# Attention and two gated mixers on one core: the first batch's q, k and the token weights loaded as rows, float64 weights rounded by an integer add, a new order for the first stage

## The chip, the core and the metric

The kernel runs on one core of a Trainium2 chip, as one program. A core has TensorE (PE in the profile; its weight loads are PEld), VectorE (DVE), ScalarE (ACT), GpSimd (POOL) and SyncE (SP), which here issues nearly all DMAs. Each engine works through its own instructions in the order in which they were recorded, and waits on semaphores for the others. The metric is the time of one execution on the device in microseconds (us), median of several runs.

## The reference

Eight batches, eight heads, 576 tokens, head dimension 64. Attention runs inside chunks of 64 tokens; its output is the input of a gated mixer with a token weight of 576x576, and that feeds a second mixer. Cut to what matters:

```python
scores = scale * np.matmul(q_c, k_c.transpose(0, 1, 2, 4, 3))   # chunks of 64 tokens
attn = softmax(scores); out = np.matmul(attn, v_c)
x = out.transpose(0, 2, 1, 3).reshape(B, S, H * D)
h = np.maximum(x @ w_in, 0.0); u, v = h[..., :512], h[..., 512:]
v_n = (v - mean(v)) / np.sqrt(var(v) + 1e-06)
v_s = np.einsum('ts,bsd->btd', w_spatial, v_n) + b_spatial[None, :, None]
x = (u * v_s) @ w_out
# second mixer: tokens (w_tok1, w_tok2), then channels (w_ch1, w_ch2), both with a residual
```

`w_in`, `w_out`, `w_tok1`, `w_tok2`, `w_ch1`, `w_ch2` come as float64; `q`, `k`, `v`, `w_spatial`, `b_spatial` as float32.

## The kernel before

All large products run on TensorE with each float32 operand split into a high and a low part (`split`, `to_hi` and `to_lo`), in three passes (`PASSES`). The first half of the program does, batch by batch, attention (class `Attn`) and the gated mixer (class `Gate`); the second half does the second mixer for all batches.

The order of the first half is written out by hand in tables of words, played one after the other: `FIRST` (batch 0's attention, batch 0's gate, and batch 1's attention, with the weights' conversion in between), then six times `STEADY` (gate of batch b beside attention of batch b+1), then `LAST`. One word is one step, and a step's instructions go onto their engines' queues in that order. The words that matter here, with an `a` ahead for batch 0's attention:

- `l`, `v`: loads of q and k, and of v, for a pair of heads. In the load of q and k a tile takes 32x32 blocks: 8 DMAs a pair, each with runs of 32 floats. `x`: VectorE turns the blocks (L322, L323; four instructions a pair).
- `S`, `s`, `e`, `n`, `z`, `T`, `t`, `P`, `p`, `q`: scores on TensorE (L336, L345); maximum and subtraction on VectorE (L355, L356); exponential on ScalarE (L362); sums and reciprocals on VectorE (L366 to L368); the scaling on GpSimd (L372); the turn of the probabilities on TensorE (L380) and their copy on ScalarE (L388); the product with v (L404, L412); its high part on ScalarE (L423, L433) and low part on VectorE (L425, L437).
- `Y`, `V`: v half of `x @ w_in` (L479; L508 for the last tokens). `R`, `r`, `F`, `G`, `rs`, `rq`, `N`, `i`, `Q`: its copies out of PSUM, the statistics (L531), the normalization (L545) and the high and low parts (L551, L560). `U`, `E`: the u half (L568) and its copy (L578). `W`: the product with the token weight (L591). `M`, `H`, `J`, `A`, `B`, `O`, `D`: the gate and the product with `w_out` (L601 to L625).
- `wl`, `wa`, `wm`, `we`, `wi`, `wj`, `wk`: load, conversion and split of one of the 12 float64 pieces of `w_in` and `w_out`. `cl`, `ca`, `cm`, `ce`, `cs`: the same conversion, in `STEADY`, of the 33 pieces of the second mixer's weights, which are stored as float32 for later.
- `gl`, `gt`, `gh`: load of the token weight in 32x32 blocks (L240, 20 DMAs), its turn on VectorE (L250), its split (L83 on ScalarE, L84 on GpSimd).
- `Z`: matmuls on zeros (L1124).

A float64 number is read as two 32-bit words. `conv_start` scales both on ScalarE (L143, L144), `conv_mid` shifts the exponent and puts in the sign on VectorE (L152, L154) and makes a power of two of the result's size (L156), and `conv_end` multiplies the low word by that and adds it, two GpSimd instructions (L164, L165).

`ps_mm` has two tiles of two PSUM banks each (tag `mm`), which the steps `Y`, `V`, `U`, `W`, `O` take in turn; `ps_at` has one tile each for scores (`s`), turned probabilities (`t`) and the product with v (`p`). A step that needs a tile waits until the last reader of the one before is done. The raw tiles of float64 pieces (`craw`) are two.

Of the kernel before, what the change touches and what calls it, by code (L numbers as in the profile page):

```python
# [21 lines left out]


FIRST = """
al0 ax0 Z9 wl0 al1 wa0 aS0 as0 wl1 ae0 an0 ax1 az0 wm0 aT0 we0 wa1 wm1 at0 we1 aS1 al2 Z3 as1
av0 ax2 ae1 an1 Z3 al3 az1 aP0 wi0 av1 ap0 ax3 wi1 wk0 aq0 aS2 aT1 at1 Y0 wl2 aP1 wl3 as2 ae2
wj1 aS3 av2 an2 wa2 wl4 wa3 az2 wm2 ap1 aq1 as3 we2 wa4 ae3 wm3 av3 aT2 an3 wi2 wl5 at2 Y1 aS4
gl0 as4 L0 wl6 wk2 aP2 ap2 gt0 az3 aq2 L1 ae4 aT3 at3 we3 an4 az4 wm4 x0 wa5 wm5 wi3 aP3 wk3
ap3 Y2 aT4 at4 wa6 we4 S0 aq3 aP4 Y3 we5 wm6 ap4 x1 wi4 R0 R1 wk4 aq4 r0 R3 s0 R2 r3 wl7 wi5
V2 wa7 gl1 gl2 we6 F S1 wk5 wl8 e0 wi6 U0 wm7 G r2 gl3 R4 we7 gl4 r1 r4 wa8 rs rq wk6 n0 z0 U1  # L30
E0 N0 T0 gt4 gh0 s1 i0 Q0 gt1 gh4 U2 wi7 N1 N2 t0 wk7 E1 L2 e1 i1 x2 P0 N4 i2 gh1 n1 p0 gt2 L3
U3 S2 i4 z1 wl9 Q1 gt3 gh2 N3 E2 gh3 i3 Q2 T1 Q3 Q4 W0 t1 E3 s2 wm8 wa9 W1 we8 x3 e2 M0 M1 wi8
wm9 q0 S3 W2 n2 wl10 we9 H0 wa10 W3 M2 s3 H2 wi9 J0 wl11 M3 z2 P1 S4 wk8 H1 J1 wj9 p1 q1 J2 H3
# [22 lines left out]
def attention_gmlp_mixer(  # L56
# [15 lines left out]
    nc = tc.nc  # L72
    NB, NH, S, D = q.shape
    DM = 512
    HALF = S // 2
    NF = w_ch1.shape[1] // 128
    scale = 1.0 / float(D) ** 0.5

    def f32(ap):
        return ap.bitcast(F32)  # L80

    def split(hi, lo, x, eng=nc.vector):
        nc.scalar.copy(out=hi, in_=x)  # L83
        eng.tensor_tensor(out=lo, in0=x, in1=f32(hi), op=ALU.subtract)  # L84
# [10 lines left out]
    lp = pool("left", side="left")  # L95
    rp = pool("right", side="right")
# [18 lines left out]

    def conv_load(src, raw=None):

        nr, n = src.shape[0], src.free_size()  # L120
# [16 lines left out]
    def conv_start(raw):  # L137
        if raw.dtype == F32:
            return raw, raw
        nr, n = raw.shape[:2]  # L140
        low, high = raw[:, :, 0], raw[:, :, 1]
        t = rp.tile([128, DM], F32, tag="ctmp", bufs=3, name="ctmp")[:nr, :n]
        nc.scalar.activation(out=t, in_=f32(high), func=ACTF.Copy, scale=2.0 ** -112)  # L143
        nc.scalar.activation(out=f32(low), in_=low, func=ACTF.Copy, scale=2.0 ** -52)  # L144
        return raw, t

    def conv_mid(raw, t):
        if raw.dtype == F32:
            return
        low, high = raw[:, :, 0], raw[:, :, 1]  # L150
        tu = t.bitcast(U32)
        nc.vector.tensor_scalar(  # L152
            out=tu, in0=tu, scalar1=3, scalar2=None, op0=ALU.logical_shift_left)
        nc.vector.scalar_tensor_tensor(  # L154
            out=tu, in0=high, scalar=0x80000000, in1=tu, op0=ALU.bitwise_and, op1=ALU.bitwise_or)
        nc.vector.tensor_scalar(  # L156
            out=high, in0=tu, scalar1=0xFF800000, scalar2=None, op0=ALU.bitwise_and)

    def conv_end(raw, t):

# [61 lines left out]
    ws_raw = {}  # L222

    def load_ws(m):
        if m == 4:

            both = lp.tile([128, 2, S], F32, tag="g0", bufs=1, name="ws_raw")
            ws_raw[4] = both[:, 0:1].rearrange("p o (t i) -> p o t i", i=32)
            ws_raw[5] = both[:, 1]
            for r in (64, 96):  # L230
                nc.sync.dma_start(
                    out=both[r:r + 1, 1], in_=b_sp.rearrange("(o s) -> o s", o=1))
        elif m % 2 == 0:

            ws_raw[m] = rp.tile([128, 2, 18, 32], F32, tag="xt", bufs=6, name="ws_raw")
            ws_raw[m + 1] = ws_raw[m]
        raw = ws_raw[m][:, m % 2]
        for a in range(4):
            e = 4 * m + a if m < 4 else 16 + a % 2
# [5 lines left out]
    ws_nat = {}

    def trans_ws(m):
        raw = ws_raw.pop(m)[:, m % 2].rearrange("p t i -> p (t i)")
        ws_nat[m] = lp.tile([128, S], F32, tag="x2o", bufs=2, name="ws_nat")
        nc.vector.transpose(out=ws_nat[m], in_=raw)  # L250

    def split_ws(m):
        nat = ws_nat.pop(m)
        if m < 4:
            split(ws_t[0][:, m], ws_t[1][:, m], nat, nc.gpsimd)
            return
        nc.scalar.copy(out=ws_r1, in_=nat)
        nc.vector.tensor_tensor(
            out=ws_r2[0:64], in0=nat[0:64], in1=f32(ws_r1[0:64]), op=ALU.subtract)

        bt = ws_raw.pop(5)
        nc.scalar.copy(out=ws_r2[64:65], in_=bt[64:65])
        nc.scalar.copy(out=ws_r2[96:97], in_=bt[96:97])
        nc.vector.tensor_tensor(
            out=ws_r2[96:97], in0=bt[96:97], in1=f32(ws_r2[96:97]), op=ALU.subtract)


    class Attn:
# [523 lines left out]
    raws = {}  # L792
# [345 lines left out]
    class Stream:
# [24 lines left out]
        "gl": load_ws, "gt": trans_ws, "gh": split_ws})  # L1163
# [171 lines left out]
```

## Time and profile before

| | us |
|---|---|
| median of 3 runs (1256.14 to 1257.96) | 1257.33 |
| the profiled execution: its time | 1259.11 |
| the profiled execution: its span | 1257.3 |
| busy in the span: PE / DVE / ACT / POOL | 1190.9 / 923.6 / 496.6 / 213.1 |

The span is from the first to the last instruction of the program; 1.8 us of the profiled execution lie around it, and it took 1.8 us more than the median. PE is busy for 95% of the span. The rows below are from three kinds of answers: busy time by stretch, waits, and instructions in order of time, each with its start, its duration and in brackets how long its engine had been idle and who released it.

### The profile page before, as it was taken

Reading aid. Unit: us, or ns where it says so; the run is one execution under the profiler, and the core shown is the slowest. Engines: PE = TensorE matmul, PEld = TensorE weight load, DVE = VectorE, ACT = ScalarE, POOL = GpSimd, SP = SyncE. Lnnn points to the kernel's source line nnn. Section 1 sums busy time; section 2 is a strip of 40 time slices with the busy share of each in tenths; the row PEclk is TensorE's granted clock in tenths of the full one; section 3 lists DMA queues with packets and bytes.
Section 4 is the critical chain, followed back from the end, with each engine's and each line's share of the span. In section 5 each row is a group of like instructions: output and inputs, shape, how many; then the busy total and the mean of one; then the engine's idle time right before and its main releaser. Section 6 shows DMA issues by size and latency. Waiting matters only on the chain. (4 is left out here: it accounts for less than half of the span.)

```text
span 1257.3 us, 25171 instructions
## 1 busy us (share of the span) xinstructions
PE 1190.9 (95%) x9983; PEld 1123.0 (89%) x9983; DVE 923.6 (73%) x1427; ACT 496.6 (39%) x786; POOL 213.1 (17%) x205
## 2 busy tenths in 40 slices
PE   6689999999998999999889999999998999999997
PEld 4588998989797988898779899999998999999997
DVE  6897767687776868366686776767768977877786
ACT  2564535354544536244332332232225433333331
POOL 2644122222323231105220000000005100000000
PEclk9989999999999999999999999999999999999999
DMA  9956446374739383157545665565376576666663
GB/s 162 186 111 130 86 120 116 94 172 103 183 78 202 58 195 81 72 106 210 151 139 166 183 178 180 152 171 192 141 276 202 208 208 192 185 192 196 207 212 46
DMA packets 426362, 196.16 MB, mean 156 GB/s; under 512 B 369666, under 2 KB 389570, under 8 KB 426244
## 3 DMA queue, kind: packets, MB, share of 16 engines
q1 hardware_dynamic: 421380, 193.96, 58.9%
q8 instruction: 78, 1.28, 0.4%
q10 hardware_dynamic: 4864, 0.59, 0.3%
q14 instruction: 40, 0.33, 0.1%
HBM read 123.31 MB, written 71.17 MB: 155 GB/s over the span
## 5 line engine op out<-in xcount | busy, mean ns | idle before, releaser
L953 PE MATMUL ps_c<-ub,wt 128*128 128x288 f32 x2016 | 289.3, 299 | 7.8 <-DVE u L982 2.5
L953 PEld LDWEIGHTS ps_c<-ub,wt 128*128 128x128 f32 x2016 | 278.2, 191 | 14.0 <-ACT s L985 3.6
L953 PE MATMUL ps_c<-hb,wt 128*128 128x288 f32 x2016 | 269.1, 295 | 1.6 <-DVE hb L1042 1.5
L953 PEld LDWEIGHTS ps_c<-hb,wt 128*128 128x128 f32 x2016 | 268.2, 188 | 2.4 <-DVE hb L1042 2.3
L591 PE MATMUL ps_s<-ws,vn 128*128 128x288 f32 x768 | 110.9, 301 | 2.9 <-ACT ut L578 2.8
L1041 ACT CAST hb<-h 128x1728 fp32r<-128x1728 f32 x40 | 64.8, 1638 | 123.0 <-DVE h L1034 42.9
L591 PEld LDWEIGHTS ps_s<-ws,vn 128*128 128x128 f32 x768 | 105.9, 193 | 4.5 <-ACT ut L578 4.3
L617 PE MATMUL ps_o<-g,w_out 128*128 128x288 f32 x768 | 107.6, 297 | 0.7 <-DVE w_out L190 0.7
L568 PE MATMUL ps_u<-xt,w_in 128*128 128x288 f32 x768 | 107.9, 300 | 0.0
L568 PEld LDWEIGHTS ps_u<-xt,w_in 128*128 128x128 f32 x768 | 105.5, 193 | 0.9 <-POOL w_in L190 0.2
L617 PEld LDWEIGHTS ps_o<-g,w_out 128*128 128x128 f32 x768 | 102.6, 188 | 2.5 <-DVE w_out L190 0.9
L1042 DVE TENSOR_TENSOR hb<-h,hb 128x1728 fp32r<-128x1728 f32 x40 | 78.2, 1955 | 28.9 <-ACT hb L1041 28.9
L479 PE MATMUL ps_v<-w_in,xt 128*128 128x512 f32 x384 | 94.8, 404 | 2.7 <-ACT xt L423 1.3
L479 PEld LDWEIGHTS ps_v<-w_in,xt 128*128 128x128 f32 x384 | 72.8, 192 | 21.1 <-ACT xt L423 1.5
L372 POOL TENSOR_TENSOR e<-e,sm 128x512 f32<-128x512 f32 (+1 forms) x40 | 38.9, 972 | 226.9 <-DVE sm L368 153.7
L869 PE MATMUL ps_u<-w,h 128*128 128x288 f32 x384 | 61.8, 298 | 4.5 <-DVE xh L874 4.5
L910 ACT CAST ub<-xh 128x576 fp32r<-128x576 f32 x56 | 37.4, 672 | 70.0 <-DVE xh L917 66.8
L869 PEld LDWEIGHTS ps_u<-w,h 128*128 128x128 f32 x384 | 54.7, 190 | 5.7 <-DVE xh L874 5.6
L164 POOL TENSOR_TENSOR craw<-craw 128x512 f32<-128x512 f32 (+3 forms) x41 | 40.1, 978 | 116.0 <-DVE craw L156 34.0
L911 DVE TENSOR_TENSOR ub<-xh,ub 128x576 fp32r<-128x576 f32 x56 | 43.1, 770 | 21.1 <-ACT ub L910 20.6
L811 ACT CAST xn<-nat 128x512 fp32r<-128x512 f32 x40 | 24.8, 619 | 79.2 <-DVE nat L809 74.6
L830 PE MATMUL ps_h<-xn,w 128*128 128x512 f32 x192 | 51.2, 400 | 3.5 <-ACT xn L811 3.5
(145 smaller groups left out, 1697.9 us busy)
## 6 DMA issues: line engine op xcount, KB each, us to landing
hd<-c SPq DMA_DIRECT2D x120, 288.0 KB, 2.5
h<-hd SPq DMA_DIRECT2D x40, 864.0 KB, 6.7
craw<-in_moe_w_ch_dram SPq DMA_DIRECT2D x24, 512.0 KB, 4.8
x_raw<-x2d SPq DMA_DIRECT2D x160, 64.0 KB, 2.6
qk_raw<-in_q_dram SPq DMA_DIRECT2D x128, 72.0 KB, 4.2
qk_raw<-in_k_dram SPq DMA_DIRECT2D x128, 72.0 KB, 3.1
xh<-x2d SPq DMA_DIRECT2D x16, 576.0 KB, 5.6
u2d<-xh SPq DMA_DIRECT2D x16, 576.0 KB, 3.1
```

Source lines behind the costliest of these rows:

```text
L164: nc.gpsimd.tensor_tensor(out=f32(high), in0=f32(low), in1=f32(high), op=ALU.mult)
L372: nc.gpsimd.tensor_tensor(out=e, in0=e, in1=sm.to_broadcast([128, e.shape[1], 64]), op=ALU.mult)
L479: nc.tensor.matmul(ps, lhsT=self.xt[kc][:, p, 128 * ti:128 * ti + 128], rhs=w_in_t[r][:, kc, DM:2 * DM], start=kc == 0 and n == 0, stop=kc ...
L568: nc.tensor.matmul(ps[:, h, 0:HALF], lhsT=w_in_t[r][:, kc, 128 * m:128 * m + 128], rhs=self.xt[kc][:, p, HALF * h:HALF * h + HALF], start= ...
L591: nc.tensor.matmul(ps[:, h, 0:HALF], lhsT=lhsT, rhs=rhs[:, HALF * h:HALF * h + HALF], start=n == 0, stop=n == len(ops) - 1)
L617: nc.tensor.matmul(ps[:, h, 0:HALF], lhsT=w_out_t[r][:, kc, 128 * m:128 * m + 128], rhs=self.g[p][:, kc, h], start=kc == 0 and n == 0, sto ...
L830: nc.tensor.matmul(ps[kk], lhsT=PB["w1"][r][:, m, ksl], rhs=xn[:, p], start=m == 0 and n == 0, stop=False)
L869: nc.tensor.matmul(ps, lhsT=h1[:, kk, p, 128 * m:128 * m + 128], rhs=PB["w2"][r][:, kk, HALF * h:HALF * h + HALF], start=n == 0, stop=n == 5)
L911: eng.tensor_tensor(out=lo, in0=x, in1=f32(hi), op=ALU.subtract)
L953: nc.tensor.matmul(ps, lhsT=lhsT, rhs=rhs, start=first and n == 0, stop=n == len(ops) - 1, skip_group_check=True)
L1041: nc.scalar.copy(out=hi, in_=x)
L1042: nc.vector.tensor_tensor(out=lo, in0=x, in1=f32(hi), op=ALU.subtract)
```

## The change

Three things change, all in code that runs during the first half:

1. Batch 0's q and k come as rows (`load_rows`): 128 tokens by 64 floats, runs of 64 floats, 4 DMAs a pair of heads and 2 more for the last tokens, in place of 32. The turn is made by TensorE (`turn`, eight matmuls with the identity a pair) into a `mm` tile, and ScalarE copies it out (`turned`, word `y`, two copies a pair). The later batches keep the blocks. The token weight also comes as rows (`load_ws`, 3 DMAs and 2 for the bias in place of 22); TensorE turns it (`turn_ws`, 25 matmuls in five steps into the `p` tile), and its low part is made by VectorE straight from PSUM.
2. The conversion from float64: the low word is scaled by another power of two and written as an integer, VectorE's third instruction goes, and GpSimd's two become one integer add. This touches all 45 pieces, 12 in `FIRST` and 33 in `STEADY`.
3. `FIRST` is put in a new order, and the large raw tiles (`g0`, `g1`) now hold pieces 0 to 3 rather than 4 to 7; the words `Z3` are gone. The last three lines of the table stay nearly as they were.

The core of the diff; of the table one line of each stands for all:

```diff
-al0 ax0 Z9 wl0 al1 wa0 aS0 as0 wl1 ae0 an0 ax1 az0 wm0 aT0 we0 wa1 wm1 at0 we1 aS1 al2 Z3 as1
+al0 wl0 al1 wl1 Z9 ax0 ay0 wa0 aS0 as0 ax1 al2 av0 wl2 wm0 ae0 ay1 an0 we0 az0 aS1 as1 wa1 aT0 wi0 wm1
...
-        nc.scalar.activation(out=f32(low), in_=low, func=ACTF.Copy, scale=2.0 ** -52)
+        nc.scalar.activation(out=low, in_=low, func=ACTF.Copy, scale=2.0 ** -29)
...
-        nc.vector.tensor_scalar(
-            out=high, in0=tu, scalar1=0xFF800000, scalar2=None, op0=ALU.bitwise_and)
...
-        nc.gpsimd.tensor_tensor(out=f32(high), in0=f32(low), in1=f32(high), op=ALU.mult)
-        nc.gpsimd.tensor_tensor(out=t, in0=t, in1=f32(high), op=ALU.add)
+        tu = t.bitcast(U32)
+        nc.gpsimd.tensor_tensor(out=tu, in0=tu, in1=raw[:, :, 0], op=ALU.add)
...
+    def turn_ws(m):
+        ps = ps_at.tile([128, 2, 8, 64], F32, tag="p", bufs=1, name="ps_w")
+        ps = ws_ps[m] = ps.rearrange("p a c q -> p (a c q)")
+        for c in range(5):
+            n = 128 if c < 4 else 64
+            nc.tensor.transpose(
+                ps[0:128 if m < 4 else 64, 128 * c:128 * c + n],
+                ws_rows[c][0:n, 128 * m:min(128 * m + 128, S)], ident[0:n, 0:n])
...
     def split_ws(m):
-        nat = ws_nat.pop(m)
+        ps = ws_ps.pop(m)[:, 0:S]
         if m < 4:
-            split(ws_t[0][:, m], ws_t[1][:, m], nat, nc.gpsimd)
+            split(ws_t[0][:, m], ws_t[1][:, m], ps)
...
+            for src in (q, k):    # load_rows
...
+                for h2 in range(2):
+                    nc.sync.dma_start(
+                        out=raw[:, :, h2],
+                        in_=src[b, 2 * hp + h2, 0:512, :].rearrange("(c p) d -> p c d", p=128))
...
+        def turn(self, u):
+            ps = self.qk[u] = ps_mm.tile([128, 2, 512], F32, tag="mm", name="ps_x")
...
+                        nc.tensor.transpose(
+                            ps[:, n, 128 * c:128 * c + 128],
+                            raw[n][:, c].rearrange("p h d -> p (h d)"), ident)
...
+        def turned(self, u):
...
+                nc.scalar.copy(out=ts[n], in_=ps[:, n])
...
-        if 4 <= i < 8:
+        if i < 4:
```

Where this moves instructions, at three places. First, VectorE in the third round of `STEADY` (the first where both pieces are whole ones of 128x512), from the conversion of two pieces (`ctmp`, `craw`) to the statistics of v. Before:

```order
L152 TENSOR_SCALAR ctmp<-ctmp 128x512
L154 SCALAR_TENSOR_TENSOR ctmp<-craw,ctmp 128x512
L156 TENSOR_SCALAR craw<-ctmp 128x512
L152 TENSOR_SCALAR ctmp<-ctmp 128x512
L154 SCALAR_TENSOR_TENSOR ctmp<-craw,ctmp 128x512
L156 TENSOR_SCALAR craw<-ctmp 128x512
L531 BN_STATS st<-v_3249 128x6
```

The same place now:

```order
L153 TENSOR_SCALAR ctmp<-ctmp 128x512
L155 SCALAR_TENSOR_TENSOR ctmp<-craw,ctmp 128x512
L153 TENSOR_SCALAR ctmp<-ctmp 128x512
L155 SCALAR_TENSOR_TENSOR ctmp<-craw,ctmp 128x512
L588 BN_STATS st<-v_3227 128x6
```

Two of six instructions ahead of the statistics are gone; nothing else moved there.

Second, TensorE in `FIRST` from the end of batch 0's v product (`ps_v`) to its u product (`ps_u`); `ps_s` are batch 1's scores. Before:

```order
L508 MATMUL ps_v<-w_in_84,xt 128x512
L508 MATMUL ps_v<-w_in_85,xt 64x512
L508 MATMUL ps_v<-w_in_84,xt 128x512
L508 MATMUL ps_v<-w_in_85,xt 64x512
L508 MATMUL ps_v<-w_in_84,xt 128x512
L508 MATMUL ps_v<-w_in_85,xt 64x512 x2
L508 MATMUL ps_v<-w_in_84,xt 128x512
L336 MATMUL ps_s<-qkT_706,qkT_703 64x64 x16
L568 MATMUL ps_u<-xt,w_in_84 128x288 x2
```

The same place now:

```order
L246 MATMUL ps_w<-ident,ws_rows 128x128 x4
L246 MATMUL ps_w<-ident,ws_rows 128x64
L391 MATMUL ps_s<-qkT_665,qkT_662 64x64 x16
L565 MATMUL ps_v<-w_in_84,xt 128x512
L565 MATMUL ps_v<-w_in_85,xt 64x512
L565 MATMUL ps_v<-w_in_84,xt 128x512
L565 MATMUL ps_v<-w_in_85,xt 64x512
L565 MATMUL ps_v<-w_in_84,xt 128x512
L565 MATMUL ps_v<-w_in_85,xt 64x512 x2
L565 MATMUL ps_v<-w_in_84,xt 128x512
L246 MATMUL ps_w<-ident,ws_rows 128x128 x4
L246 MATMUL ps_w<-ident,ws_rows 128x64
```

Two of the five turns of the token weight (`ps_w`) stand here, and batch 1's first scores come ahead of L565 rather than, as before, ahead of the end of the v product.

Third, ScalarE at the same place of `FIRST`: the copies of v out of PSUM (`v_162` to `v_166`, `v_sum`), a piece's high part (`w_in_84`), the token weight's (`ws_88`). Before:

```order
L526 ACTIVATE v_162<-ps_v 128x512
L526 ACTIVATE v_163<-ps_v 128x512
L526 ACTIVATE v_165<-ps_v 128x512
L526 ACTIVATE v_164<-ps_v 128x512
L187 CAST w_in_84<-ctmp 128x4x128
L143 ACTIVATE ctmp<-wu_raw 128x512
L144 ACTIVATE wu_raw<-wu_raw 128x512
L517 COPY v_sum<-ps_v 64x512
L518 COPY v_sum<-ps_v 64x512
```

The same place now:

```order
L583 ACTIVATE v_162<-ps_v 128x512
L583 ACTIVATE v_163<-ps_v 128x512
L83 CAST ws_88<-ps_w 128x576
L583 ACTIVATE v_165<-ps_v 128x512
L185 CAST w_in_84<-ctmp 128x4x128
L574 COPY v_sum<-ps_v 64x512
L575 COPY v_sum<-ps_v 64x512
L417 ACTIVATE e<-e 128x512
L583 ACTIVATE v_164<-ps_v 128x512
```

The copy of `v_164`, which is the last reader of its `mm` tile, was fourth in a row and now stands behind a piece's high part, the copies for `v_sum` and an exponential.

## Rows read from the trace of the kernel before

**Rows 1.** Busy time by stretch: PE, PEld, DVE, ACT, POOL, clock, DMA, GB/s.

```profile
0.00:54.40 54.40, 35.85 (x401) 26.73 (x401) 40.33 (x75) 21.45 (x40) 25.48 (x27) 0.94 0.93 171
54.40:81.90 27.50, 20.16 (x208) 17.81 (x208) 26.23 (x52) 20.34 (x34) 14.81 (x13) 0.97 0.87 168
119.20:255.00 135.80, 135.12 (x1405) 124.68 (x1394) 92.81 (x200) 59.89 (x120) 24.89 (x30) 1.00 0.51 111
255.00:525.00 270.00, 257.77 (x2627) 238.64 (x2627) 196.64 (x379) 124.69 (x228) 75.29 (x66) 0.99 0.56 129
```

**Rows 2.** What TensorE waited for from 119.2 to 525 us.

```profile
PE ps_t L380 <- POOL e L372: 4.4, 4, 1.1
PE ps_s L336 <- DVE last L323: 4.4, 4, 1.8
```

**Rows 3.** In order of time, STEADY's fourth round: start, duration, engine, instruction.

```profile
316.58 0.69 DVE L154 SCALAR_TENSOR_TENSOR ctmp<-craw,ctmp 128x512 uint32<-128x512 uint32 x1
...
325.29 1.43 DVE L154 SCALAR_TENSOR_TENSOR ctmp<-craw,ctmp 128x512 uint32<-128x512 uint32 x1
...
326.83 0.43 DVE L156 TENSOR_SCALAR craw<-ctmp 128x512 uint32<-128x512 uint32 x1
...
327.34 1.15 POOL L164 TENSOR_TENSOR craw<-craw 128x512 f32<-128x512 f32 x1 [1.16 <-DVE craw L156]
...
327.63 1.41 DVE L154 SCALAR_TENSOR_TENSOR ctmp<-craw,ctmp 128x512 uint32<-128x512 uint32 x1
...
329.14 1.34 DVE L156 TENSOR_SCALAR craw<-ctmp 128x512 uint32<-128x512 uint32 x1
...
330.40 0.69 DVE L531 BATCH_NORM_STATS2 st<-v 128x6 f32<-128x512 f32 x1
...
331.74 1.30 POOL L165 TENSOR_TENSOR ctmp<-ctmp,craw 128x512 f32<-128x512 f32 x1
...
336.47 1.15 PE L336 MATMUL ps_s<-qkT,qkT 64*64 64x64 f32 x32 [1.47 <-DVE last L323]
...
338.73 0.66 PE L380 MATMUL ps_t<-ident,e 128*128 128x128 f32 x4 [1.10 <-POOL e L372]
```

**Rows 4.** TensorE in order of time, the third round, same place.

```profile
268.12 1.15 PE L336 MATMUL ps_s<-qkT,qkT 64*64 64x64 f32 x32 [0.25 <-DVE last L323]
```

**Rows 5.** TensorE in order of time, FIRST.

```profile
2.69 4.21 PE L1124 MATMUL ps_w<-zeros 128*128 128x512 f32 x9 [2.69 <-DVE zeros L1118]
...
7.87 1.97 PE L336 MATMUL ps_s<-qkT,qkT 64*64 64x64 f32 x32 [0.98 <-DVE qkT L322]
...
51.34 3.06 PE L479 MATMUL ps_v<-w_in,xt 128*128 128x512 f32 x12
...
72.59 0.69 PE L404 MATMUL ps_p<-aT,vt 64*64 64x64 f32 x32 [0.95 <-ACT aT L388]
...
80.68 1.11 PE L380 MATMUL ps_t<-ident,e 128*128 128x128 f32 x4 [2.70 <-POOL e L372]
81.91 5.68 PE L591 MATMUL ps_s<-ws,vn 128*128 128x288 f32 x24
...
87.95 3.36 PE L591 MATMUL ps_s<-ws,vn 128*128 128x288 f32 x24
```

**Rows 6.** Groups by line and form, 0 to 119.2 us: busy, mean ns.

```profile
L322 DVE STREAM_TRANSPOSE qkT<-qk_raw 128x512 f32<-128x512 f32 x18 | 12.5, 693 | 5.0 <-DMA qk_raw<-in_k_dram 2.9 <-DMA qk_raw<-in_q_dram 2.2
L143 ACT ACTIVATE ctmp<-craw 128x512 f32<-128x512 f32 x8 | 5.4, 674 | 17.7 <-DMA craw<-in_moe_w_in_dram 14.1 <-DMA craw<-in_moe_w_out_dram 3.6
L388 ACT COPY aT<-ps_t 128x512 f32<-128x512 f32 x8 | 4.6, 581 | 3.3 <-PE ps_t L380 3.3
L250 DVE STREAM_TRANSPOSE ws_nat<-ws_raw 128x576 f32<-128x576 f32 x5 | 3.8, 763 | 2.0 <-DMA ws_raw<-in_moe_w_spatial_dram 2.0
L601 DVE TENSOR_TENSOR ut<-ps_s,ut 128x576 f32<-128x576 f32 x4 | 3.0, 748 | 2.9 <-PE ps_s L591 2.9
L355 DVE TENSOR_REDUCE mx<-ps_s 128x8 f32<-128x512 f32 x8 | 5.4, 676 | 2.0 <-PE ps_s L336 1.9
```

More of the change, by code (lines that the diff above doesn't have):

```diff
@@ L220, in attention_gmlp_mixer @@
                   for c in range(0, w.shape[1], DM)]
[L222 to L239, printed above, removed]
-            nc.sync.dma_start(
-                out=raw[32 * a:32 * a + 32],
-                in_=w_sp[:, 32 * e:32 * e + 32].rearrange("(t j) i -> j t i", j=32),
-            )
@@ L245, in attention_gmlp_mixer, with load_ws @@
[L245 to L250, printed above, removed]
+    ws_rows = {}
+    def load_ws(i):
+        if i < 2:
+            t = rp.tile([128, 2, S + 64], F32, tag="xt", bufs=6, name="ws_rows")[:, :, 0:S]
+            nc.sync.dma_start(
+                out=t, in_=w_sp[256 * i:256 * i + 256].rearrange("(c p) n -> p c n", p=128))
+            for c in range(2):
+                ws_rows[2 * i + c] = t[:, c]
+            return
+        ws_rows[4] = lp.tile([128, S], F32, tag="x2o", bufs=2, name="ws_rows")
+        nc.sync.dma_start(out=ws_rows[4][0:64], in_=w_sp[512:576])
+        for r in (64, 96):
+            nc.sync.dma_start(
+                out=ws_rows[4][r:r + 1], in_=b_sp.rearrange("(o s) -> o s", o=1))
@@ L254, in split_ws @@
         if m < 4:
-            split(ws_t[0][:, m], ws_t[1][:, m], nat, nc.gpsimd)
+            split(ws_t[0][:, m], ws_t[1][:, m], ps)
             return
-        nc.scalar.copy(out=ws_r1, in_=nat)
+        for h in range(2):
+            nc.scalar.copy(out=ws_r1[64 * h:64 * h + 64], in_=ps[0:64])
         nc.vector.tensor_tensor(
-            out=ws_r2[0:64], in0=nat[0:64], in1=f32(ws_r1[0:64]), op=ALU.subtract)
-        bt = ws_raw.pop(5)
+            out=ws_r2[0:64], in0=ps[0:64], in1=f32(ws_r1[0:64]), op=ALU.subtract)
@@ L300, in load_qk, with load_rows @@
             self.raw[hp] = raws
+        def load_rows(self, hp):
+            b = self.b
+            raws = []
+            for src in (q, k):
+                raw = rp.tile([128, 18, 32], F32, tag="raw", bufs=4, name="qk_rows")
+                raw = raw.rearrange("p t i -> p (t i)")[:, 0:512].rearrange(
+                    "p (c h d) -> p c h d", c=4, h=2)
+                for h2 in range(2):
+                    nc.sync.dma_start(
+                        out=raw[:, :, h2],
+                        in_=src[b, 2 * hp + h2, 0:512, :].rearrange("(c p) d -> p c d", p=128))
+                raws.append(raw)
+            self.raw[hp] = raws
+            if hp == 3:
+                raw = lp.tile([128, S], F32, tag="x2o", bufs=2, name="qk_rows")
+                raw = raw[:, 0:512].rearrange("p (h d) -> p h d", h=8)
+                for n, src in enumerate((q, k)):
+                    nc.sync.dma_start(
+                        out=raw[64 * n:64 * n + 64],
+                        in_=src[b, :, 512:576, :].rearrange("h p d -> p h d"))
+                self.raw[4] = raw
@@ new lines, in turn @@
+        def turn(self, u):
+            ps = self.qk[u] = ps_mm.tile([128, 2, 512], F32, tag="mm", name="ps_x")
+            raw = self.raw.pop(u)
+            for n in range(2):
+                if u < 4:
+                    for c in range(4):
+                        nc.tensor.transpose(
+                            ps[:, n, 128 * c:128 * c + 128],
+                            raw[n][:, c].rearrange("p h d -> p (h d)"), ident)
+                else:
+                    r = slice(64 * n, 64 * n + 64)
+                    for hp in range(4):
+                        nc.tensor.transpose(
+                            ps[:, n, 64 * hp:64 * hp + 64],
+                            raw[r, 2 * hp:2 * hp + 2].rearrange("p h d -> p (h d)"),
+                            ident[r, r])
@@ new lines, in turned @@
+        def turned(self, u):
+            ps = self.qk.pop(u)
+            if u == 4:
+                for n in range(2):
+                    nc.scalar.copy(
+                        out=self.last[n].rearrange("p h d -> p (h d)"), in_=ps[:, n, 0:256])
+                return
+            self.qk[u] = ts = [rp.tile([128, 512], F32, tag=f"qkT{n}", bufs=2, name=f"qkT{n}")
+                               for n in range(2)]
+            for n in range(2):
+                nc.scalar.copy(out=ts[n], in_=ps[:, n])
@@ L456, in ops @@
                        q=lambda u: self.put(u, 1))
+            if self.b == 0:
+                ops.update(x=self.turn, y=self.turned)
             return {pre + n: fn for n, fn in ops.items()}
```

27 lines of the change are left out of this document (16 added, 11 removed).

## The prediction

> **What bounds the kernel now.** I read busy time by stretch first. From 119.2 to 255 us TensorE is busy for 135.1 of 135.8 us: nothing that frees another engine can be seen there. From 255 to 525 us it idles for 12.2 us, and in the first stage, up to 54.4 us and from there to 81.9 us, for 18.6 and 7.3 us [rows 1]. So the change can act at two places: the first stage, and the last four rounds of STEADY. Then the waits of the second: of its idle time, 4.4 us are for VectorE's turn of q and k, and 4.4 us for GpSimd's scaling, four times each, once a round [rows 2]. Then the instructions around one such wait, in order of time. The reader is to see a row of VectorE work without a gap: from the second L154 at 327.63 over L156 at 329.14 to L531 at 330.40 and on to the turn that releases TensorE at 336.47, 1.47 us late; then TensorE waits 1.10 us more for the scaling that follows [rows 3]. In this place VectorE sets TensorE's time.
>
> In the first stage no engine is full up to 54.4 us (VectorE 40.3, TensorE 35.9, ScalarE 21.5); the chain from step to step and the DMAs bound it, ScalarE alone waiting 14.1 us for pieces of w_in [rows 1, 6]. From 54.4 to 81.9 us VectorE is busy for 26.2 of 27.5 us [rows 1]: there it is the bound.
>
> **The conversion in STEADY.** 33 times VectorE loses L156 and GpSimd's L164 and L165 become one add. What a round gains is the shift of L531. The first L154 ends at 326.72 in both. Before, L156 follows, and L164 can begin only behind it, at 327.34; the second L154 stands beside it and takes 1.41 us, not the 0.69 it takes alone; the second L156 stands beside L165 and takes 1.34 us, not 0.43 [rows 3]. Now the add begins at 326.8. Its price isn't in the trace: GpSimd has no integer instruction. The nearest rows are L165 (1.30, the same tiles and strides, an add) and L164 (1.04 to 1.15); the far end is that it costs as much as both together, 2.35. I take 1.30, as the row with the same operation and operands. Then it ends at 328.1, the second L155 needs the 0.55 us that its forerunner needed behind L164's end (328.49 to 329.04), and L531 begins at 328.75, not 330.40: 1.65 us. TensorE's two waits in that round add up to 2.57 us, so all of it counts. In the third round the two waits are 0.25 and, as in every round, 1.1 us [rows 2, 4]: at most 1.35 there. The rounds five and six have the other 4.9 us of the 8.8 [rows 2], more than a shift of 1.65 each can use up. Sum: 1.35 + 3 x 1.65 = **6.3 us**. At 1.04 a piece it would be 7.1; at 2.35 L531 moves by only 0.6, and the sum is 2.4. What is late next: the scaling, still by some 0.9 us a round.
>
> That the add blocks VectorE is the row's reading: 1.41 beside a GpSimd instruction, 0.69 without. The Trainium skill ("GPSIMD Engine Reference", section Key points) says that GpSimd shares its SBUF interfaces with VectorE, and that instructions with two SBUF inputs or in a two-port mode contend; the trace agrees. By that rule the add holds L155 back as L164 did, which the sum has in it; without it L155 would end 0.7 us sooner, and the sum would be 8.
>
> ScalarE's L145 now writes integers. No row has that; L144 reads them at the speed of L143 (0.67). Bounds: 0.58, as a plain copy, and 1.35, twice as much; I take 0.67 and no change, since ScalarE is busy for 125 of 270 us there [rows 1, 6].
>
> **The first stage, to the end of the v product.** It ends at 54.40 before [rows 5]. Now: the nine matmuls on zeros stay and end at 6.9; the first turn is eight matmuls at the half-clock price of L380 (1.11 for four), to 9.1; a copy of 0.58; first scores at 9.9, two us later than the 7.87 of before [rows 5, 6]. From pair to pair: scores 1.15, maximum and subtraction 2 x 0.68, exponential about a copy's 0.6, two copies 1.16, and one piece's two scalings 1.35, which stand between them on ScalarE: 5.6 us [rows 3, 6]. So the fourth pair's scores are at 26.7. To the first Y: 1.15 + 1.36 + 0.6, two half copies 0.6, two scalings 1.35 and a cast 0.6, a copy 0.58, P 0.69 and the last scores 0.6: 7.5, at 34.2. From there TensorE has all it needs: four Y of 3.06 and two T and two P in between, about 2.2: the end is at 48.7, **5.7 us ahead**. The DMAs aren't in this chain: q and k need 18 DMAs, not 32, the token weight 5, not 22, and ScalarE's 14.1 us of waiting go [rows 6]. Of the moved loads, piece 6 stands ahead of batch 1's second pair on SP's queue and waits there for a raw tile, until piece 4 is converted at about 45; the pair's blocks are wanted at 60.
>
> **From there to the gate's W.** W begins at 81.91 before, 27.5 us behind the v product [rows 5]. TensorE's 20.2 us grow by 25 turns at 0.165 (L380 at full clock, 0.66 for four: 4.1) and by batch 1's first scores (1.15), which were earlier before: 25.5 [rows 1, 3]. If nothing waited, W would begin at 74.2. But VectorE's 26.2 us hardly shrink: less five turns at 0.76 (3.8) and one L156 (0.4), plus four low parts from PSUM at 0.75 as L601 (3.0) and the blocks of one more pair (1.8): 26.8 [rows 3, 6]. 1.5 of it can be done under the v product; the next VectorE instruction waits for the first turn and its high part on ScalarE, until 50.2. Five more times VectorE waits for ScalarE, which itself stands behind something: behind the v_164 copy, behind the square root, behind the table load of the exponential. I price each at 1.3, a copy and a cast with their handoffs: 6.5. So 50.2 + 25.3 + 6.5 = 82.0, then scores and T (1.8) and W at **84, 2 us late**. Where the waits queue up: on ScalarE a cast waits for GpSimd's add of piece 5, and behind it stand the v_sum copies and v_164, whose tile the first U needs: TensorE idles some 3 us there, and some 4 before the last U, whose tile ScalarE frees behind the cast of piece 7.
>
> Behind W: its 5.68 us ran at half clock, against 3.36 for the next one [rows 5]; TensorE had idled 2.7 us before it. If the clock is up, 2.3 come back; as the idle times are as long now, I count half, 1.2. The first stage: 2.1 - 1.2, **1 us later** than before. Bounds: 7.7 sooner (nothing waits), and 11 later (below).
>
> The Trainium skill speaks against the turns ("TensorE: Matmul & The Clock Gate", Part 4: PE-mode transpose): about 275 ns for one in a kernel's context. The rows have four in 0.66 us, so 0.165 each. By the page's figure the 25 turns would be 6.9 and not 4.1, an estimate, and W 2.8 us later.
>
> **The sum**, against the profiled execution's own 1259.11 us: - 6.3 + 1 = 1253.8. That execution was 1.8 above the median of 1257.33, so **1252**.
>
> **Rivals.**
> - The lead stays: ScalarE answers in time and W begins at 75 to 76. For it: TensorE needs only 25.5 us. Against: VectorE's 26.8 us in one queue. First stage -7, in all 1244.
> - The add costs as much as the two instructions it replaces. For it: GpSimd is the slow engine, 1.30 for what VectorE does in 0.69 [rows 3]. Against: same operation, same tiles. STEADY gains 2.4, the first stage loses 1: 1256.
> - Slower: TensorE's idle times before the first and the last U each pull its clock down, as the 2.7 us before W did [rows 5], and U, U and W run at half: 3 x 3.4 = 10 us more and W near 91. With STEADY's gain of 6.3 that is 1262 or, with the 1 us, above. It decides from the point where W begins later than 88 (81.9 + 6.3). Against it: VectorE, not TensorE, leads there, and hides part of a slow U.
> - The change does not do what it says where TensorE is full: up to 255 us the conversion is worth nothing; that is in the sum.
>
> **How the numbers follow.** The forecast 0.52 (its own range 1248 to 1256), the lead kept 0.20, the dear add 0.12, slower 0.12, anything else 0.04. Below 1244 and above 1259 lies a part of the second and of the fourth, some 0.15 in all: the range is 1244 to 1259. Within 0.2% (2.5 us, about what a measurement of this kernel can tell from no change) is a tenth of the forecast, half of the dear add and some of the slower case: 0.16; slower 0.12; faster 0.72.
>
> **What would show it.** The add's row near 1.3 us; L588 one and a half us sooner behind the two conversions; TensorE's waits for the turn of q and k gone from 255 to 525 us and those for the scaling below 1 us; the v product ending near 49; the first U waiting for the copy of v_164; W at 84. Wrong: W before 78 or after 88, an add above 2 us, or waits of TensorE in STEADY that stay 8.8 us, since then something behind VectorE's queue set them.

## The result, and the profile after

| | before | changed |
|---|---|---|
| median (lowest to highest, 5 runs), us | 1257.33 (1256.14 to 1257.96) | 1243.20 (1242.91 to 1244.85) |
| span of the profiled execution, us | 1257.3 | 1242.3 |
| busy PE / DVE / ACT / POOL, us | 1190.9 / 923.6 / 496.6 / 213.1 | 1192.9 / 879.5 / 501.0 / 161.7 |

The ratio is 0.9887 with a 95% interval of 0.9874 to 0.9899: 14.1 us faster. The forecast was 1252, 5.3 faster, with a range of 1244 to 1259; the result lies just below it. The direction, and STEADY's last four rounds as the main place, were right; the size was not.

Busy time by stretch of the changed kernel answers to [rows 1] (same columns):

```profile
0.00:54.40 54.40, 39.45 (x453) 31.98 (x453) 30.55 (x62) 27.39 (x54) 19.88 (x22) 0.91 0.88 194
54.40:81.90 27.50, 21.13 (x145) 19.69 (x146) 20.96 (x41) 16.77 (x28) 7.74 (x6) 0.77 0.51 84
119.20:255.00 135.80, 135.10 (x1373) 124.53 (x1370) 90.22 (x195) 59.72 (x117) 19.50 (x22) 1.00 0.57 119
255.00:525.00 270.00, 268.21 (x2712) 248.38 (x2711) 180.03 (x367) 131.28 (x238) 48.40 (x42) 1.00 0.53 128
```

The last row is the one that moved: TensorE is busy for 268.2 of 270 us, where it was 257.8. TensorE's only wait of more than a moment from 119.2 to 525 us is now this one (waiting line, releaser, total, times, longest); the two of [rows 2] are gone, not smaller:

```profile
PE ps_s L648 <- ACT ut L635: 2.5, 6, 0.6
```

The start of the v product marks each round of STEADY. From these rows of TensorE (start, duration) the gain can be placed:

| v product of batch | 1 | 2 | 3 | 4 | 5 | 6 | 7 |
|---|---|---|---|---|---|---|---|
| before, us | 120.25 | 184.75 | 249.13 | 316.21 | 385.63 | 453.34 | 520.79 |
| changed, us | 119.45 | 183.92 | 248.30 | 312.69 | 377.10 | 441.71 | 505.23 |
| ahead by | 0.80 | 0.83 | 0.83 | 3.52 | 8.53 | 11.63 | 15.56 |

So 0.8 us come from the first stage and 14.7 from the last four rounds of STEADY (2.7, 5.0, 3.1 and 3.9 by round), and 0.6 is lost again in the rest, where nothing was changed.

STEADY's fourth round of the changed kernel, in order of time, answers to [rows 3]:

```profile
311.48 0.40 SPq L130 DMA_DIRECT2D craw<-in_moe_w_ch_dram  x1
...
311.68 0.69 DVE L155 SCALAR_TENSOR_TENSOR ctmp<-craw,ctmp 128x512 uint32<-128x512 uint32 x1
312.51 1.30 POOL L163 TENSOR_TENSOR ctmp<-ctmp,craw 128x512 uint32<-128x512 uint32 x1 [4.67 <-DMA x2d<-x2o]
312.69 11.40 PE L536 MATMUL ps_v<-w_in,xt 128*128 128x512 f32 x48
...
314.24 0.46 SPq L130 DMA_DIRECT2D craw<-in_moe_w_ch_dram  x1
...
316.03 0.66 ACT L144 ACTIVATE ctmp<-craw 128x512 f32<-128x512 f32 x1 [3.62 <-DMA craw<-in_moe_w_ch_dram]
...
317.80 0.69 DVE L421 TENSOR_REDUCE sm<-e 128x8 f32<-128x512 f32 x1 [2.65 <-ACT e L417]
...
319.25 1.44 DVE L155 SCALAR_TENSOR_TENSOR ctmp<-craw,ctmp 128x512 uint32<-128x512 uint32 x1
...
320.82 1.37 POOL L163 TENSOR_TENSOR ctmp<-ctmp,craw 128x512 uint32<-128x512 uint32 x1 [0.68 <-DVE ctmp L155]
321.06 1.68 DVE L155 SCALAR_TENSOR_TENSOR ctmp<-craw,ctmp 128x512 uint32<-128x512 uint32 x1
...
322.66 0.68 DVE L588 BATCH_NORM_STATS2 st<-v 128x6 f32<-128x512 f32 x1
...
331.25 1.10 PE L391 MATMUL ps_s<-qkT,qkT 64*64 64x64 f32 x32
```

From the first conversion of the pair to the statistics it is 3.41 us (319.25 to 322.66), where it was 5.11 (325.29 to 330.40): 1.70 less, and the prediction had 1.65. But the statistics stand 9.97 us behind the v product's start, and they stood 14.19 behind it: 4.2 us sooner. The other 2.5 lie ahead of the pair. These rows of before, of the same round and of the end of the one ahead of it, show where:

```profile
292.64 10.43 SPq L215 DMA_DIRECT2D c_f<-ctmp  x2
...
301.39 1.30 POOL L165 TENSOR_TENSOR ctmp<-ctmp,craw 128x512 f32<-128x512 f32 x1
...
314.87 0.64 ACT L624 COPY x2o<-ps_o 128x576 f32<-128x576 f32 x1 [4.60 <-DMA x2d<-x2o]
...
315.95 1.76 SPq L215 DMA_DIRECT2D c_f<-ctmp  x1
...
317.76 0.42 SPq L129 DMA_DIRECT2D craw<-in_moe_w_ch_dram  x1
...
319.05 1.31 POOL L165 TENSOR_TENSOR ctmp<-ctmp,craw 128x512 f32<-128x512 f32 x1
...
320.77 0.42 SPq L129 DMA_DIRECT2D craw<-in_moe_w_ch_dram  x1
...
322.08 0.66 ACT L143 ACTIVATE ctmp<-craw 128x512 f32<-128x512 f32 x1 [4.91 <-DMA craw<-in_moe_w_ch_dram]
...
323.19 0.62 ACT L362 ACTIVATE e<-e 128x512 f32<-128x512 f32 x1
...
323.84 0.69 DVE L366 TENSOR_REDUCE sm<-e 128x8 f32<-128x512 f32 x1 [3.27 <-ACT e L362]
...
325.54 0.67 ACT L143 ACTIVATE ctmp<-craw 128x512 f32<-128x512 f32 x1 [1.74 <-DMA craw<-in_moe_w_ch_dram]
```

The reader is to see a chain through ScalarE and SyncE, read from its end. VectorE waits 3.27 us for the exponential before it comes to the pair at all (323.84). The exponential stands behind ScalarE's two scalings of the pair's first piece, and ScalarE stands 4.91 us for that piece's load (322.08). This is the load issued at 317.76: asked of it alone, the trace gives 4.2 us to landing, and ScalarE's 4.9 us as the wait that it ends. The load at 320.77, behind GpSimd's end at 320.36, is that of the pair's second piece (325.54) and not in this chain.

The first load stands on SyncE's queue behind a store of 1.76 us, that one behind a store of the gate's output, and this waits for ScalarE's copy at 314.87, which had itself stood 4.60 us until an earlier output's store was through. Further ahead the queue was held by two stores, from 292.64 to 303.07, the second of them until GpSimd had ended its piece (302.69); from there to 312.57 SyncE's issues follow each other without a gap (one of them waits for VectorE until 307.64). So the conversion is in the time twice: in the pair's own row on VectorE, and in SyncE's queue, which waits for GpSimd to end the pieces before. Of those, the second piece of the pair before took 4.00 us from its L154 to the end of L165 (298.69 to 302.69), and takes 2.43 now (294.50 to 296.93). That end lies 13.52 us ahead of the v product before and 15.76 now; the first load is issued 1.55 us behind the v product before and 1.21 ahead of it now (311.48). Of these 2.8 us, 1.4 are ScalarE's copy, which comes sooner (from 1.34 to 2.76 ahead of the v product), and 1.4 the store between, which took 1.76 and now 0.38; the trace names no wait of that store, and why it was long stays open. Whether the queue counts by itself, the runs below test.

### The profile page after: what moved, and what is told of

It is laid out like the page before. It is cut to its first block, busy times and chain, and to the rows that moved or that the text cites. A ratio compares the mean times of both kernels' runs of the same rounds, so it can differ in the third digit from the quotient of the medians.

```text
span 1242.3 us, 25079 instructions
## 1 busy us (share of the span) xinstructions
PE 1192.9 (96%) x10042; PEld 1127.6 (91%) x10042; DVE 879.5 (71%) x1365; ACT 501.0 (40%) x797; POOL 161.7 (13%) x156
## 5 line engine op out<-in xcount | busy, mean ns | idle before, releaser
L1010 PEld LDWEIGHTS ps_c<-ub,wt 128*128 128x128 f32 x2016 | 278.2, 190 | 12.9 <-ACT s L1042 3.8
L1010 PEld LDWEIGHTS ps_c<-hb,wt 128*128 128x128 f32 x2016 | 268.2, 188 | 2.2 <-DVE hb L1099 2.2
L163 POOL TENSOR_TENSOR ctmp<-ctmp,craw 128x512 uint32<-128x512 uint32 (+3 forms) x41 | 49.6, 1211 | 135.4 <-DVE ctmp L155 64.6
```

Source lines behind the costliest of these rows:

```text
L163: nc.gpsimd.tensor_tensor(out=tu, in0=tu, in1=raw[:, :, 0], op=ALU.add)
L1010: nc.tensor.matmul(ps, lhsT=lhsT, rhs=rhs, start=first and n == 0, stop=n == len(ops) - 1, skip_group_check=True)
```

## The experiments

Theory A: the conversion counts twice, in VectorE's row and through the loads, which SyncE issues late because its queue waits for GpSimd's end. Theory B: VectorE's row alone, as predicted, and the rest of the gain is the first stage's. All ratios are against the kernel before on the same chip.

**One part alone.** The kernel before with the diff's conversion and nothing else:

```diff
-  nc.vector.tensor_scalar(out=high, in0=tu, scalar1=0xFF800000, ...)   # and the two GpSimd ops
+  nc.gpsimd.tensor_tensor(out=tu, in0=tu, in1=raw[:, :, 0], op=ALU.add)     # and ScalarE's scale
```

> The kernel before with the new conversion alone; the first stage keeps its order and its loads in blocks. Theory A (the conversion counts twice): each piece is converted 1.65 us sooner, and in STEADY this stands ahead of VectorE's statistics two times over, once in VectorE's own row and once through the raw tile, since the load of the piece after next waits for GpSimd's last reader; TensorE's waits for the turn of q and k and for the scaling go altogether, and with them the half-clock stretches behind them. Then nearly the whole 14 us are here: 1243 to 1245. Theory B (as predicted, only VectorE's own row counts, and the rest of the gain comes from the first stage's new order and loads, which hand STEADY a better start): 6.3 us, 1250 to 1252.

Measured: 1243.84, ratio 0.9874 (0.9855 to 0.9893). The whole gain is the conversion's: the interval and that of the changed kernel (0.9874 to 0.9899) overlap.

**The other part alone.** The changed kernel with the old conversion put back:

```diff
-  nc.gpsimd.tensor_tensor(out=tu, in0=tu, in1=raw[:, :, 0], op=ALU.add)
+  nc.gpsimd.tensor_tensor(out=f32(high), in0=f32(low), in1=f32(high), op=ALU.mult)
+  nc.gpsimd.tensor_tensor(out=t, in0=t, in1=f32(high), op=ALU.add)         # and VectorE's mask
```

> The changed kernel with the old conversion: first batch's q, k and the token weight as rows, and the new order of the first stage. Theory A: STEADY is as before, and only the 0.8 us by which the first stage ended sooner remain; its own 12 pieces are again converted by the longer way, which may cost the first stage 1 to 3 us: 1256 to 1260. Theory B: some 8 us of the gain are the first stage's: 1248 to 1250.

Measured: 1263.99, ratio 1.0041 (1.0026 to 1.0055), slower, and by somewhat more than A had. The loads as rows and the new order are a loss by themselves. The first v product of STEADY says it by stage: 120.25 us before, 117.36 with the conversion alone, 124.21 with the rows and the order alone, 119.45 with all: rows and order cost 4.0 us with the old conversion and 2.1 with the new. The conversion alone gains 2.9 us there and 14.1 more in STEADY (v product of batch 7 at 503.77, before at 520.79). B's second half falls.

**Which instruction.** GpSimd keeps a first instruction; then VectorE keeps its third:

```diff
+  nc.gpsimd.tensor_tensor(out=f32(high), in0=f32(low), in1=f32(high), op=ALU.mult)
   nc.gpsimd.tensor_tensor(out=tu, in0=tu, in1=low, op=ALU.add)
```

> The kernel before with the new conversion, but GpSimd keeps its first instruction (the multiplication, whose result nobody reads) ahead of the integer add, so it holds the raw tile as long as before; VectorE's third instruction is gone. Theory A: the load of the piece after next comes about as late as before less 0.5 us a piece, so most of the gain is lost: 1250 to 1254. Theory B (VectorE's own time): VectorE's row is rid of its third instructions, 0.43 and 1.34 us, and the gain stays that of the new conversion alone, within 1.5 us.

Measured: 1250.92, ratio 0.9934 (0.9910 to 0.9959): half of the gain is lost. The five times lie between 1247.08 and 1254.88, and the trace is that of the slowest.

```diff
+  nc.vector.tensor_scalar(out=high, in0=tu, scalar1=0xFF800000, ...)
```

> The kernel before with the new conversion, but VectorE keeps its third instruction (the mask, whose result nobody reads); GpSimd has the one integer add. Against the new conversion alone this puts 2 x 0.43 us, or up to 1.8 beside GpSimd, back into VectorE's row, and lets the raw tile go 0.4 us later where the add waits for the mask. Theory A (both the row and the return of the raw tile count, and the scaling's lead is 0.8 us): a little of the gain is lost, 1245 to 1248. Theory B (VectorE's row alone counts): half of it, 1249 to 1252. If VectorE's instructions don't matter at all: 1243 to 1245.

Measured: 1248.34, ratio 0.9912 (0.9892 to 0.9931): at the upper end of A's numbers and just under B's, so this run does not decide. The first speaks against VectorE's row alone; it doesn't say whether GpSimd's own time or the late load did it.

**The load made late, twice too much.** To the conversion alone, first a DMA out of the raw tile that the next load must wait for, then four small copies ahead of each load:

```diff
+  nc.sync.dma_start(out=held[n], in_=raw[0:1, 0:64, 0])      # behind each store
```

> The kernel before with the new conversion, and in STEADY a DMA of 64 numbers out of each raw tile, issued behind the store of the converted piece. No engine gets an instruction more; only the next load into that raw tile must wait for this DMA, some 2 us. Theory A: the row of VectorE begins up to 2 us later in each of the last four rounds; the scaling's lead was 0.8 us, so 1.2 us of TensorE's wait come back in each, with the clock falls behind some of them: 5 to 8 us slower than the new conversion alone. Theory B: no VectorE or GpSimd instruction is added, so the time is that of the new conversion alone, within 1 us.

Measured: 1408.59. The DMA of 64 numbers took 8.9 us (median from issue to landing), not 2.

```diff
+  for _ in range(4): nc.sync.dma_start(out=held[n], in_=b_sp[0:64])   # ahead of each load
```

> The kernel before with the new conversion, and four small copies from DRAM to DRAM issued by SyncE ahead of each load of a raw tile in STEADY. Nobody waits for them; at 0.3 to 0.45 us an issue they put the load about 1.6 us later, as much as the old conversion's longer hold of the raw tile did, and no compute engine gets an instruction more. Theory A: VectorE's row begins up to 1.6 us later; the scaling leads by 0.8 us now, so up to 0.8 us of wait comes back in each of four rounds, more where loads of q and k are put later too: 1245 to 1250. Theory B (the time at which the load is issued doesn't matter): 1243 to 1245.

Measured: 1307.39. The four issues took 2.4 to 4.9 us, and SyncE's other work came late with them: ScalarE waited 36.6 us, four times, for the stores of the gate's output (9.7 with the conversion alone). Both are on A's side in sign, and neither is a dose that can be read: the queue carries too much else.

**The load made early.** A better handle: in STEADY the stores stood ahead of the loads (`cs cs cl cl`), so one load waited for the other piece's GpSimd work too. With the load first, two runs: in one GpSimd's second instruction comes behind the add and squares the converted tile (so the weights are other numbers), in the other it comes ahead of the add, as above:

```diff
-cs cs cl cl L5 ...
+cl cl cs cs L5 ...
```

> The kernel before with the new conversion; GpSimd gets a second instruction behind the integer add, on the converted tile alone (it squares it, so the weights are other numbers), and in STEADY each load stands ahead of the store beside it on SyncE's queue. GpSimd works as long as in the run with two instructions, but the raw tile is free after the first. Theory A (the return of the raw tile counts as much as VectorE's row): most of what that run lost against the new conversion alone (1250.9 against 1243.8) is back, 1244 to 1247. Theory B (it lost by GpSimd's time and by what VectorE suffers beside it): 1249 to 1252.

Measured: 1242.55, ratio 0.9873 (0.9859 to 0.9888).

> The control of the run before: the same order of loads and stores, and GpSimd's two instructions with the unused multiplication ahead of the add, so that the raw tile is held to the end of the second. Both theories: 1249 to 1252, as without the new order; if it is near 1245, the order of loads and stores was what counted.

Measured: 1244.20, ratio 0.9889 (0.9873 to 0.9906). So which of the two instructions held the raw tile hardly counted; the order on SyncE's queue did. The last run has the same instructions on ScalarE, VectorE and GpSimd as the one with 1250.92, and is 6 us faster. The first piece's load, its scaling and the exponential in the fourth round, first with the stores first (v product at 314.66), then with the loads first (312.45):

```profile
315.48 0.45 SPq L129 DMA_DIRECT2D craw<-in_moe_w_ch_dram  x1
...
320.42 0.66 ACT L143 ACTIVATE ctmp<-craw 128x512 f32<-128x512 f32 x1 [4.16 <-DMA craw<-in_moe_w_ch_dram]
...
321.54 0.62 ACT L361 ACTIVATE e<-e 128x512 f32<-128x512 f32 x1
```

```profile
310.88 0.38 SPq L129 DMA_DIRECT2D craw<-in_moe_w_ch_dram  x1
...
315.42 0.67 ACT L143 ACTIVATE ctmp<-craw 128x512 f32<-128x512 f32 x1 [3.25 <-DMA craw<-in_moe_w_ch_dram]
...
316.56 0.61 ACT L361 ACTIVATE e<-e 128x512 f32<-128x512 f32 x1
```

The load begins 0.82 us behind the v product in the one and 1.57 ahead of it in the other, the exponential 6.88 and 4.11 behind it, and VectorE's statistics 13.51 and 9.58: 2.8 of the 3.9 us lie ahead of the exponential.

**The load early, and nothing else,** on the kernel before:

> The kernel before, with the old conversion and the old first stage; in STEADY each load of a raw tile stands ahead of the store beside it on SyncE's queue, and nothing else is changed. Theory A' (what counted is when the next load is issued, since VectorE's row begins when it has landed; the store that waits for GpSimd stood ahead of it): 1245 to 1251, without one instruction less on any engine. Theory B (the gain is the instructions that VectorE and GpSimd no longer have): 1256 to 1259.

Measured: 1254.23, ratio 0.9963 (0.9950 to 0.9977): 4.7 us by the ratio, between the two expectations. The load's time counts by itself, and is a third of the gain by itself; the rest needs fewer instructions. Neither theory alone; what the runs fit is a limit that both work on. From the traces of these runs, the start of the first exponential and of the first statistics behind the v product, and the time from this v product to the next:

| round | exponential | statistics | next v product |
|---|---|---|---|
| changed, 3 / 4 / 5 | 2.6 / 4.5 / 4.8 | 8.6 / 10.0 / 10.7 | 64.4 / 64.4 / 64.6 |
| conversion alone, 4 | 5.9 | 11.4 | 65.3 |
| two on GpSimd, 3 | 5.1 | 11.7 | 66.7 |
| load first, old conversion, 4 | 5.2 | 12.5 | 67.6 |
| before, 3 / 5 / 4 | 5.7 / 6.3 / 7.0 | 12.9 / 13.6 / 14.2 | 67.1 / 67.7 / 69.4 |

From the exponential to the statistics it is 7.2 us before and with the load first, and 5.5 to 6.0 with the new conversion: the order on SyncE's queue moves the first part alone (1.7 us in round 4), the conversion moves both (2.5 and 1.7). Up to about 11 us a round takes 64.4, TensorE's own time; behind that each us costs one or more. The change moved the statistics of rounds 3 to 6 by 2.9 to 4.4 us, across that edge; a shift of 1.65 would have left them at 11.3 to 12.8, behind it. (The sixth round, the last of STEADY, is not in the table: there a round falls below 64.4, to 63.5 in the changed kernel at 10.8.)

**The first stage.** Two waits that the prediction named are taken away in the changed kernel, one word and then some more:

```diff
-R3 we5 gt1 wi5 F r1 e0 R2 r3
+R3 R2 we5 gt1 wi5 F r1 e0 r3
```

> The changed kernel with one word of the first stage moved: ScalarE copies v_164 out of PSUM right behind v_165, ahead of the cast that waits for GpSimd. If that copy is what holds the first U (3.18 us of TensorE's idle time, and then 4.98 us for 24 matmuls that take 3.46 at full clock), U begins near 52 instead of 55.25; what VectorE does behind it sets W, so W comes only 0 to 3 us sooner: 1240 to 1243. If the first stage's end is set elsewhere: 1243.

Measured: 1244.58, ratio 0.9879 (0.9862 to 0.9896), no change that the runs can tell from the changed kernel. U began at 50.30 instead of 55.25, as expected, and W at 83.83 instead of 85.20; TensorE waited for VectorE twice instead (1.76 and 1.58 us).

```diff
-wa7 i0 Q0 t0 e1 gh3 N1 U2 wm7 n1 N2 we7 gt4 i1 wi7 E1 z1 Q1 gh4 wk7
+wa7 i0 Q0 wm7 t0 E1 gh3 we7 N1 e1 U2 wi7 gt4 N2 i1 n1 wk7 z1 Q1 gh4
```

> The same, and the last piece of the u half of w_in is shifted on VectorE ahead of the token weight's low part and cast on ScalarE ahead of an exponential, and the copy that frees the last U's tile goes ahead of that cast. TensorE waited 3.33 and 1.20 us there and ran at half clock up to 81 us. If those two places hold the first stage, the last U begins near 72 instead of 75 to 77, W near 80 instead of 85.2, and the whole is 1237 to 1241, faster than the new conversion alone (1243.84 on the other chip, 14.9 below its before). If VectorE's row sets W anyway: 1242 to 1244.

Measured: 1238.30, ratio 0.9827 (0.9809 to 0.9846), clear of the changed kernel's interval. In TensorE's rows the last U and W came when expected:

```profile
72.49 3.18 PE L625 MATMUL ps_u<-xt,w_in 128*128 128x288 f32 x22 [0.46 <-POOL w_in L188]
...
79.94 4.54 PE L648 MATMUL ps_s<-ws,vn 128*128 128x288 f32 x24
```

A further order of that stage, against the run before:

```diff
-F r1 e0 r3 wa6 G r2 gh1 wk5 U0 wl7 n0 x1 R4 z0 wm6 gt2 r4 we6 rs rq gh2 wi6 S1 U1 E0
+F gh1 r1 e0 x1 wa6 r3 G r2 wk5 U0 gt2 wl7 wm6 S1 n0 R4 z0 we6 r4 gh2 wi6 U1 E0 rs rq
```

> The changed kernel with the two waits less (1238.3), and a further order of the first stage: VectorE makes the token weight's second low part and turns batch 1's second pair ahead of the statistics, and shifts piece 6 ahead of the sums; ScalarE casts piece 6 ahead of the square root. TensorE waited 1.76 and 1.58 us there and ran its second u product at half clock (5.34 us). If those waits go, the last U begins 4 to 6 us sooner, and W, which VectorE's row still sets, 1 to 4 us sooner: 1234 to 1238. If VectorE's row alone sets W: 1238.

Measured: 1240.51, ratio 0.9857 (0.9840 to 0.9873). U's second product began at 57.57 instead of 61.15, but W at 80.02, as in the run before, which fits the expectation that VectorE's row sets it. Not better.

**Both findings together,** the two waits less and the loads first:

> The changed kernel with the two waits less in the first stage, and each load ahead of the store beside it in STEADY. With the new conversion TensorE's waits for VectorE and GpSimd in STEADY are gone already, so the second finding has only the 2.8 us of waits for ScalarE's copy of u to act on: 1236 to 1239, at most 2 us under the first finding alone (1238.3).

Measured: 1236.77, ratio 0.9819 (0.9791 to 0.9846): 21 us under the kernel before on the same chip, and the fastest of all; what the loads first add to 1238.30 lies inside the intervals.

## Why the prediction was wrong, point by point

**The step that failed** is in the conversion in STEADY: "The first L154 ends at 326.72 in both." It held everything ahead of the pair fixed. The view of one wait, read from the second L154 on, showed a row of VectorE work without a gap, and so a bound that seemed to begin there; the same view read four us further back has VectorE idle for 3.27 us, and follows to a load that SyncE issued late, on a queue that waits for GpSimd. The row's own part was sized rightly, 1.70 us; the 2.5 us ahead of it were put at nothing. The shift was 4.2 us in that round, not 1.65, and so TensorE's waits of 8.8 us all went, where 6.3 were forecast.

**Not priced at all:** the clock behind those waits. [Rows 1] had 0.99 for 255 to 525 us; in finer stretches (columns as in [rows 1]):

```profile
406.00:410.00 4.00, 2.89 (x26) 2.75 (x22) 2.02 (x7) 3.03 (x6) 1.04 (x1) 0.72 1.36 206
410.00:414.00 4.00, 4.00 (x28) 4.00 (x28) 3.53 (x7) 2.80 (x6) 0.00 (x0) 0.86 0.83 124
474.00:478.00 4.00, 2.90 (x41) 2.76 (x40) 2.59 (x8) 2.66 (x5) 1.04 (x1) 0.75 1.29 237
478.00:482.00 4.00, 4.00 (x27) 4.00 (x27) 3.03 (x6) 2.87 (x6) 0.00 (x0) 0.82 0.66 121
```

Behind TensorE's idle times in the rounds five and six its clock stood at half (1.2 GHz) for some 7 us: 4 x (0.28 + 0.14 + 0.25 + 0.18) = 3.4 us of lost time. In the changed kernel the rounds have 1.00 throughout. Also not priced: a 1.3 us wait of a v product for ScalarE's copy of the gate's output, gone too. Sum from the traces: 10.4 us less idle (12.2 to 1.8) and 3.4 of clock, 13.8 of the 14.7; the last us is not placed.

**What held.** The add's price: 1.30 taken, 1.315 in the mean of 26 rows of STEADY. So the rival of a dear add falls. VectorE's row: 1.65 taken, 1.70 read. That the add blocks VectorE: L155 takes 1.68 beside it, 0.69 alone; by the Trainium skill ("GPSIMD Engine Reference", section Key points) that is the shared SBUF interface, and the trace agrees again.

**The first stage** came out 0.8 us sooner, 1 later was forecast. TensorE's rows answer to [rows 5]:

```profile
6.70 1.63 PE L334 MATMUL ps_x<-ident,qk_rows 128*128 128x128 f32 x8
9.48 1.15 PE L391 MATMUL ps_s<-qkT,qkT 64*64 64x64 f32 x32 [1.16 <-ACT qkT L355]
...
44.63 3.05 PE L536 MATMUL ps_v<-w_in,xt 128*128 128x512 f32 x12
47.51 0.80 PE L246 MATMUL ps_w<-ident,ws_rows 128*128 128x128 f32 x5
...
55.25 4.98 PE L625 MATMUL ps_u<-xt,w_in 128*128 128x288 f32 x24 [3.18 <-ACT v L583]
...
74.91 0.85 PE L625 MATMUL ps_u<-xt,w_in 128*128 128x288 f32 x2 [3.33 <-ACT ut L635]
76.95 5.65 PE L625 MATMUL ps_u<-xt,w_in 128*128 128x288 f32 x22 [1.20 <-POOL w_in L188]
...
85.20 3.46 PE L648 MATMUL ps_s<-ws,vn 128*128 128x288 f32 x24 [0.27 <-ACT ut L635]
```

First scores at 9.48 (forecast 9.9), the v product's end at 47.68 (48.7), the first U late by 3.18 us for the copy of v_164 (some 3), the last by 3.33 and 1.20 (some 4), W at 85.20 (84). So a lead of 6.7 us at the v product was a delay of 3.3 at W, lost in the engines' queues, as the prediction worked out. The turns cost 0.80 for five, 0.16 each. The size that was off lies behind W: its first product took 3.46, not 5.68, so the whole 2.2 us of clock came back and not half, and TensorE's 1.4 us of idle time between W and the next round's v product went. Of the 4.1 us by which that way became shorter (38.34 to 34.25), 0.5 is not placed. The half clock is not gone: it moved ahead of W, where 54.4 to 81.9 us has 0.77 for 0.97 before.

By the Trainium skill ("TensorE: Matmul & The Clock Gate", Part 4: PE-mode transpose) a turn in a kernel's context is about 275 ns; these rows, with 0.16 us each, don't agree.

**The rival of the kept lead** gave 1244, close to the 1243.2, by another way: W did not begin at 75 to 76. A time that fits does not show its reason; W's row does. The slower rival named the right stall and clock falls, U at 4.98 and 5.65 us; W at 85.2 stayed short of its point of 88. It priced them too high, 3.4 us each where the rows give some 1.5 and 2.5 over full clock, and counted W's half clock, which the kernel before had as well; and its 1262 is 1261 by the other sums' reckoning (1257.3 - 6.3 + 10.2).

## What to carry to other kernels

Where a wait is to be shortened, follow the chain back past the first engine that is busy without a gap, until nothing ahead of it uses what the change touches: here a conversion that ends sooner also lets SyncE's queue go on sooner, a load lands sooner, and the same saving counts again. A load that stands behind a store on an in-order queue inherits the store's wait; in this kernel putting it ahead was worth 4.7 us alone, and made a second GpSimd instruction nearly free. And a short wait of TensorE is not priced by its length alone: read the granted clock in stretches of a few us behind it.

## What the runs showed of the hardware that was not expected

A DMA of 64 numbers of 4 bytes, 8 bytes apart in one SBUF row, took 8.9 us from issue to landing in this traffic (median of 33). DRAM-to-DRAM copies of 256 bytes held SyncE 0.59 us each (median of 132, 0.49 to 2.96), where 0.3 to 0.45 had been expected. TensorE's clock fell behind two idle times in the fifth round (0.88 and 1.11, with 1.15 us of scores between them), and stayed full behind 1.47 and 1.10 in the fourth.
